# Half of a two-stage kernel's first loads issued by GpSimd, and a pair's tiles begun earlier and further apart

## The chip, the cores and the metric

The kernel runs on one core of a Trainium2 chip. The metric is the time of one execution in device microseconds. Engines: PE (TensorE, matrix products), DVE (VectorE), ACT (ScalarE), POOL (GpSimd) and SP (SyncE, which only issues transfers). Each takes its own instructions in program order and waits at an instruction whose semaphores are not yet there. SP, ACT and POOL each have a queue from which they issue DMA transfers.

## The reference

Eight batches of 576 positions, eight heads of 64. Attention runs inside chunks of 64 positions; then a low-rank mix over positions (U of 576x32, V of 32x576) and a ReLU block of width 2048 act on each position's 512 channels.

```python
def _attn_ref(q, k, v):
    B, H, S, D = q.shape            # 8, 8, 576, 64
    chunk = 64; nc = S // chunk
    q_c, k_c, v_c = (a.reshape(B, H, nc, chunk, D) for a in (q, k, v))
    scores = np.matmul(q_c, k_c.transpose(0, 1, 2, 4, 3)) / np.sqrt(D)
    scores = scores - np.max(scores, axis=-1, keepdims=True)
    attn = np.exp(scores)
    attn = attn / (np.sum(attn, axis=-1, keepdims=True) + 1e-09)
    return np.matmul(attn, v_c).reshape(B, H, S, D)

def _moe_ref(x, U, V, w_ch1, w_ch2):   # x: (8, 576, 512), heads side by side
    h = x.transpose(0, 2, 1) @ U @ V
    u = x + h.transpose(0, 2, 1)
    ch = np.maximum(u @ w_ch1, 0.0) @ w_ch2    # 512 -> 2048 -> 512
    return u + ch
```

U, V and the weights come as 64-bit floats and are rounded on the chip, by integer operations on their two words.

## The kernel before

**Tiling.** Batches go in four pairs of 1152 positions, nine tiles of 128 each. A tile's attention gives x; the low-rank mix turns x into u; three tiles form a group. For each group and each of 16 weight blocks of 128 hidden units, `hidden` (line 825) makes 12 products h (each operand is split into a high and a low part of fewer bits, three products of four), ACT and DVE make the ReLU's high and low part (lines 833 and 838), and `project_out` (line 851) adds 9 products into the three tiles' outputs. Such a *block* is 21 products of PE; there are 4 x 3 x 16 = 192. All weights stay in SBUF once they are rounded and split (lines 92 to 105, 372 and 375).

**The first part is planned.** The first pair's nine tiles, the rounding of U, V and the weights, and the first 32 blocks are written as a graph of operations (`Op`) with an engine, a cost and resources. `order` plays the graph through with these costs and gives one order of all instructions; each engine executes its share in that order. `LEAD` ranks the pieces: T tiles, U, V, W weight blocks, P the products with U, M the mixes, S the split of U. `transfer` adds a DMA issue. In this part each tile's q, k and v are loaded by SP (lines 416 and 420; v in four transfers of 64 KB: two chunks c and two halves e of the heads), after POOL's memset of v's column of ones (line 411). U comes in four transfers (lines 244 to 252), V in one (line 295). `GATES` says after which blocks the second pair's first two tiles begin in the same way; meanwhile ACT issues transfers that write the second pair's q and k to DRAM in another order (`permute`), which the later tiles read.

**The rest is an agenda.** From slot `FIRST` = 128 on, a block has four slots, and `at(s, ...)` puts work into slot s. `plan_tile` puts a later tile's steps around the slot s of its scores: its load at s - 9, the DVE transposes at s - 4, the v load at s + 1 (`Tile.load_v`, line 689), the exponentials' transpose and sums at s + 2, their way through DRAM (`put_ex`, line 737, at s + 3 and `get_ex`, line 744, at s + 6). The values (line 752) of a tile run in the slot of the next tile's scores; `chain` lists these slots, and `made[pr, t]` is the slot in which tile t's values run. `plan_proj` places the five products with U of a batch (lines 565 and 566), `plan_mix` the mixes: low rank, add, transpose, through DRAM (lines 795 and 801) and, ten slots after the start, the split (lines 814 and 815) on which the next pair's `hidden` waits. Slots before `FIRST` don't exist for the agenda; `plan_tile` moves a load or a transpose that would come earlier to `FIRST`.

Of the kernel before, what the change touches and what calls it, by code (L numbers as in the profile page):

```python
# [21 lines left out]
def kernel(  # L22
# [11 lines left out]
    nc = tc.nc  # L34
# [20 lines left out]
    XROOM = 3  # L55
    GATES = (14, 29)
    BLOCKS = [(hp, e, c) for hp in range(HP) for e in range(2) for c in range(2)]
# [74 lines left out]

    def transfer(run, kb, *after, eng="SP", us=0.5, take="", free="", gbs=232.0):
        q = "dq" if eng == "SP" else "pq"
        o = Op(eng, us, run, *after, take=take + " " + q, lat=1.2 if eng == "SP" else 2.9)
        return Op("DMA", kb * 1.024 / gbs, lambda: None, o, free=free + " " + q, lat=0.5)
# [100 lines left out]
    def u_ops():  # L237
        st = {}

        def load(z):  # L240
            if z == 0:
                words = st["words"] = wslot((10, 2 * R), U32, "uraw")
                nc.vector.memset(words[:, 4:6], 0)
                nc.sync.dma_start(words[:, 0:4], moe_U[0 : 4 * P].rearrange("(t p) r -> p t r", p=P))
                st["raw"] = words.rearrange("p t (r w) -> p t r w", w=2)
            words = st["words"]
            if z == 1:
                nc.sync.dma_start(words[0:C, 4], moe_U[4 * P : S])
            if z == 2:
                nc.sync.dma_start(words[C:P, 5], moe_U[0:C])  # L250
            if z == 3:
                nc.sync.dma_start(words[:, 6:10], moe_U[C:S].rearrange("(t p) r -> p t r", p=P))

        def spread():
            uf.append(wslot((10, 4, R), F32, "ufull"))
            nc.gpsimd.memset(uf[0][:, :, 3, :], 0.0)
            nc.scalar.copy(uf[0][:, :, 0:3, :], st["a"].unsqueeze(2).broadcast_to([P, 10, 3, R]))

        ld = None
        for z in range(4):  # L260
            ld = transfer(
                lambda z=z: load(z), (128, 16, 16, 128)[z], ld and ld.after[0], take="" if z else "w"
            )
        o, cv = rounding(Later(lambda: st["raw"]), lambda: wslot((10, R), U32, "uroom"), ld, "w", 10 * R)

        def keep():
            st["a"] = cv["a"].bitcast(F32)
            spread()

        return Op("ACT", 1.0, keep, o, take="w", free="w"), st  # L270
# [14 lines left out]
    def v_ops():  # L285
# [7 lines left out]
        def load():  # L293
            words = wslot((2 * n,), U32, "vraw")
            nc.sync.dma_start(words, moe_V.rearrange("r (b c) -> b r c", b=4))
            st["raw"] = words.rearrange("p (r w) -> p r w", w=2)
# [23 lines left out]

        ld = transfer(load, 147, take="w")
        o, _ = rounding(Later(lambda: st["raw"]), room, ld, "w", n)
# [77 lines left out]
    def load(pr, t, z):  # L400
# [12 lines left out]
        if z != "v":  # L413
            dst, src = (loaded[pr, t][0], q) if z == "q" else (loaded[pr, t][1], k)
            for r, m, b, s0 in segments(pr, t):
                nc.sync.dma_start(dst[r : r + m], src[b, :, s0 : s0 + m, :].rearrange("h s d -> s h d"))  # L416

    def load_v(pr, t, c, e):
        b, s0 = divmod(t * P + c * C, S)
        nc.sync.dma_start(  # L420
            loaded[pr, t][2][e * C : (e + 1) * C, c, :, 0:D],
# [3 lines left out]
    def attention_ops(pr, t, after=None):  # L425
# [88 lines left out]
        for c in range(2):  # L514
            for e in range(2):
                lv = transfer(
                    lambda c=c, e=e: load_v(pr, t, c, e),
                    64,
                    lv.after[0],
                    eng="SP",  # L520
                    us=0.5,
                )
# [141 lines left out]
    class Tile:  # L664
# [19 lines left out]
        def load_v(self):  # L684
            self.vn = slot(F32, "vn_" + self.n, (P, 2, HP, D))
            for c in range(2):
                b, s0 = divmod(self.t * P + c * C, S)
                for e in range(2):
                    nc.sync.dma_start(
                        self.vn[e * C : (e + 1) * C, c],  # L690
# [177 lines left out]
    def block_ops(pr, g, f, first, final, after, prev):  # L868
# [21 lines left out]
        for j in range(GT):  # L890
            d = Op("PE", 0.7, lambda j=j: out(j), c, d, take="bank" if first else "", free="h" if j == GT - 1 else "")
            if final:
                ends.append(
# [9 lines left out]

    LEAD = "T0 T1 T2 U T3 T4 W0 T5 P0 T6 V T7 T8 P1 M1 M0 W1 W2 W3 W4 W5 W6 W7 W8 W9 W10 M2 W11 W12 W13 W14 W15 S"
    STRETCHES = ((0, 0, 2), (1, 0, 4), (0, 2, 8), (1, 4, 12), (0, 8, 16), (1, 12, 16))
# [54 lines left out]
    manual.__enter__()  # L960
    for o in order():
        o.run()

# [13 lines left out]
    def at(s, *runs):  # L977
        agenda.setdefault(s, []).extend(runs)

    def plan_tile(pr, t, s, begin, end):  # L980

        a = Tile(pr, t)
        tile_of[pr, t] = a
        at(max(s - 9, begin), a.load)
        at(max(s - 4, begin), a.turn)
        at(s + 1, a.load_v)
# [13 lines left out]
    def plan_proj(pr, e, i, s):  # L1000
# [4 lines left out]
        at(s + 1, lo.run)  # L1005
        at(s + 4, product.run, *(z.run for z in rest))

    projs = {}
    tile_of = {}

    chain = [((1, t), FIRST + s) for t, s in zip(range(len(GATES), 7), (8, 18, 28, 38, 50))]
    for pr in range(1, NPAIR):
# [8 lines left out]
    for key, s in chain:  # L1021
        now = plan_tile(*key, s, FIRST, None) if key else None

# [15 lines left out]
    for pr in range(1, NPAIR):  # L1039
# [8 lines left out]
        for t in range(3):  # L1048
            plan_mix(pr, t, s + 7 + 2 * t)
        s = made[pr, 8] + 1  # L1050
        for i in range(5):
            plan_proj(pr, 1, i, s - 4 + i)
        for t in range(3, 6):
            plan_mix(pr, t, s + 7 + 2 * (t - 3))
        for t in range(6, 9):
            plan_mix(pr, t, base + NF * 4 + 6 + 8 * (t - 6))

    now = FIRST
    for pr in range(NPAIR):
# [46 lines left out]
```

## Time and profile before

| | |
|---|---|
| time, median of 3 runs | 958.88 us (956.23 to 963.89) |
| the profiled execution | 960.21 us, span 958.2 us |
| PE busy | 924.3 us, 96% |
| DVE, ACT, POOL busy | 452.5, 230.6, 1.7 us |
| DMA moved | 97.45 MB, mean 102 GB/s |
| PE's clock as granted | 0.989 of full speed over the run |

PE's busy time is modelled and includes what one product takes inside the array, so PE can be 100% busy; what counts is where it is not. In lists of waits a row gives the waiting engine and line, what it waited for, the total, the number of waits and the longest. "SPq" is SP's issue of a transfer, and "issue" stands where the trace shows no releaser.

### The profile page before, as it was taken

The numbers are of one execution on the slowest core, as the hardware profiler recorded it, in microseconds if no ns is written. First come the engines' busy times: TensorE is split into PE (matmuls) and PEld (weight loads), VectorE is DVE, ScalarE is ACT, GpSimd is POOL, SyncE is SP. The second block draws the span as 40 slices with busy tenths as digits, with TensorE's granted clock in tenths as the row PEclk, the third lists the DMA queues.
The fourth block names the chain that finished last, engine by engine and source line by source line (L and its number), as shares of the span: only waits on it lengthen the run. The fifth ranks groups of instructions, "written<-read, shape, count | busy, mean of one in ns | idle before, by whom it ended". The sixth has DMA issues, their size and how long they took to land.

```text
span 958.2 us, 16149 instructions
## 1 busy us (share of the span) xinstructions
PE 924.3 (96%) x6632; PEld 816.2 (85%) x6632; DVE 452.5 (47%) x890; ACT 230.6 (24%) x405; POOL 1.7 (0%) x18
## 2 busy tenths in 40 slices
PE   4789999999999999999999999999999999999998
PEld 3468988888888888888889888888889889899997
DVE  3669988144574455534632555543641533321211
ACT  3545655121221122112211121111221121111110
POOL 0000000000000000000000000000000000000000
PEclk8979999999999999999999999999999999999999
DMA  7792355456758634432764635442350312210000
GB/s 149 173 297 95 134 174 109 73 116 156 152 117 201 114 75 135 111 77 71 156 127 78 136 71 127 126 102 47 78 133 1 100 23 67 66 34 1 33 1 34
DMA packets 307005, 97.45 MB, mean 102 GB/s; under 512 B 239348, under 2 KB 296820, under 8 KB 306932
## 3 DMA queue, kind: packets, MB, share of 16 engines
q1 hardware_dynamic: 195572, 82.27, 33.3%
q10 hardware_dynamic: 111360, 14.16, 9.4%
q8 instruction: 52, 0.85, 0.4%
q14 instruction: 21, 0.17, 0.1%
HBM read 73.32 MB, written 37.22 MB: 115 GB/s over the span
## 4 chain that ended last, share of the span: by engine, by line
PE 88%; DMA 3%; DVE 3%; SPq 3%; ACT 1%; issue 1%; POOL 0%; DVEq 0%; ACTq 0%; POOLq 0%
PE h L825 41%; PE o L851 40%; PE as L752 2%; SPq L420 1%; PE as L699 1%; DMA qkv<-in_q_dram 1%; PE u L612 1%; PE ps_eT L433 1%; PE ut L624 1%; DMA vraw<-in_moe_V_dram 1%; PE y L566 1%; DMA wraw<-in_moe_w_ch_dram 1%; SPq L416 0%; PE av L482 0%; ACT hh L833 0%
## 5 line engine op out<-in xcount | busy, mean ns | idle before, releaser
L825 PE MATMUL h<-uth,w 128*128 128x384 f32 x1536 | 424.3, 339 | 1.3 <-ACT uth L814 1.3
L851 PE MATMUL o<-w,hh 128*128 128x512 f32 x1152 | 364.2, 397 | 0.0
L838 DVE SCALAR_TENSOR_TENSOR hl<-h,hh 128x384 fp32r<-128x384 f32 x192 | 106.9, 557 | 416.9 <-ACT hh L833 416.6
L825 PEld LDWEIGHTS h<-uth,w 128*128 128x128 f32 x1536 | 281.3, 188 | 9.6 <-ACT uth L814 1.8
L825 PE MATMUL h<-utl,w 128*128 128x384 f32 x768 | 260.0, 339 | 0.5 <-DVE utl L815 0.5
L851 PEld LDWEIGHTS o<-w,hh 128*128 128x128 f32 x1152 | 212.3, 188 | 35.9
L851 PE MATMUL o<-w,hl 128*128 128x512 f32 x576 | 227.4, 395 | 0.0
L833 ACT ACTIVATE hh<-h 128x384 fp32r<-128x384 f32 x192 | 94.3, 491 | 549.6 <-PE h L825 542.2
L825 PEld LDWEIGHTS h<-utl,w 128*128 128x128 f32 x768 | 144.3, 188 | 9.1 <-DVE utl L815 0.7
L851 PEld LDWEIGHTS o<-w,hl 128*128 128x128 f32 x576 | 108.4, 188 | 25.4
L863 DVE TENSOR_TENSOR x<-o,x 128x512 f32<-128x512 f32 x48 | 31.2, 680 | 3.4 <-PE o L851 3.4
L719 ACT ACTIVATE ex<-ex 128x512 f32<-128x512 f32 x25 | 15.8, 632 | 68.1 <-DVE ex L713 68.1
L712 DVE TENSOR_REDUCE mx<-as 128x4 f32<-128x256 f32 x50 | 20.9, 419 | 13.3 <-PE as L699 13.1
L618 DVE TENSOR_TENSOR x<-u,x 128x512 f32<-128x512 f32 x36 | 23.9, 678 | 4.7 <-PE u L612 4.7
L752 PEld LDWEIGHTS as<-vn,eT 64*64 64x64 f32 x800 | 15.5, 134 | 11.4 <-issue 10.5
L752 PE MATMUL as<-vn,eT 64*64 64x64 f32 x800 | 19.5, 225 | 2.9 <-issue 2.6
L815 DVE TENSOR_TENSOR utl<-uf,uth 128x512 fp32r<-128x512 f32 x27 | 18.5, 687 | 8.1 <-ACT uth L814 8.1
L713 DVE TENSOR_TENSOR ex<-as,mx 128x256 f32<-128x256 f32 x50 | 21.2, 425 | 1.7
L554 ACT CAST xh<-x 128x512 fp32r<-128x512 f32 x30 | 18.1, 615 | 14.4 <-DMA out_dram<-x 5.0
L375 DVE TENSOR_TENSOR w<-wroom,w 128x1024 fp32r<-128x1024 f32 (+1 forms) x19 | 20.0, 1051 | 1.3 <-ACT w L372 1.2
L372 ACT CAST w<-wroom 128x1024 fp32r<-128x1024 f32 (+1 forms) x19 | 17.2, 913 | 13.6 <-DVE wroom L105 13.5
L102 DVE SCALAR_TENSOR_TENSOR wraw<-wraw 128x1024 uint32<-128x1024 uint32 (+1 forms) x19 | 20.0, 1054 | 0.8 <-ACT wraw L95 0.8
(91 smaller groups left out, 509.7 us busy)
## 6 DMA issues: line engine op xcount, KB each, us to landing
wraw<-in_moe_w_ch_dram SPq DMA_DIRECT2D x32, 512.0 KB, 4.6
out_dram<-x SPq DMA_DIRECT2D x36, 256.0 KB, 2.2
vn<-in_v_dram SPq DMA_DIRECT2D x108, 64.0 KB, 2.4
qblocks<-in_q_dram ACTq DMA_DIRECT2D x24, 288.0 KB, 4.0
kblocks<-in_k_dram ACTq DMA_DIRECT2D x24, 288.0 KB, 3.9
xs<-xb SPq DMA_DIRECT2D x108, 64.0 KB, 1.8
uf<-xs SPq DMA_DIRECT2D x27, 256.0 KB, 2.8
exs<-exb SPq DMA_DIRECT2D x100, 64.0 KB, 1.8
```

Of the source, the lines that this page charges most:

```text
L102: lambda: nc.vector.scalar_tensor_tensor(lo, hi, 0x80000000, lo, op0=ALU.bitwise_and, op1=ALU.bitwise_or),
L375: nc.vector.tensor_sub(st["w"][:, 1, cols], v, st["w"][:, 0, cols])
L618: nc.vector.tensor_add(x, st["u"], x)
L712: nc.vector.reduce_max(mx[:, e], self.sc[e].rearrange("p (h k) -> p h k", k=C), axis=AX.X)
L713: nc.vector.tensor_sub(self.ex[:, e].rearrange("p b h k -> p h b k"), self.sc[e].rearrange("p (h b k) -> p h b k", b=2, k=TB), mx[:, e].un ...
L752: nc.tensor.matmul(ps[e][cs, (HP + hp) * C : (HP + hp + 1) * C], lhsT=self.eT[rows, hp, 2 * c : 2 * c + 2, :].rearrange("p a i -> p (a i)" ...
L815: nc.vector.tensor_sub(ul, self.uf, uh)
L825: nc.tensor.matmul(ps[:, :GN], lhsT=w[:, z, cc], rhs=u[:, cc, :], start=(n == 0), stop=(n == 3 * NCC - 1))
L833: nc.scalar.activation(hh, ps[:, :GN], AF.Relu)
L838: nc.vector.scalar_tensor_tensor(hl, ps[:, :GN], 0.0, hh, op0=ALU.max, op1=ALU.subtract)
L851: nc.tensor.matmul(acc[j], lhsT=h[:, js], rhs=w2[f][:, z], start=(first and i == 0), stop=(final and i == 2),)
L863: nc.vector.tensor_add(x, ps, x)
```

## The change

The loads of U and V, and in the first pair's tiles the two of four v transfers with c = 0, are issued on GpSimd's queue instead of SP's; so are all v transfers of the tiles on the agenda (`Tile.load_v`). The c = 0 transfers no longer stand behind k in the plan. `LEAD` takes V third and W0 later, and S before the last weights. The second gate comes five blocks earlier. The agenda now starts at slot 0 and is run between the planned blocks too, so the second pair's third tile has its scores at `FIRST` - 13, and the following tiles stand at `FIRST` + 2, 14, 27 and 42 instead of 18, 28, 38 and 50. The fifth product with U of each batch and all but a pair's last three mixes come one slot later after their tile. The planner's cost of an issue goes from 0.5 to 0.62 us.

```diff
-    GATES = (14, 29)
+    GATES = (14, 24)
...
-    def transfer(run, kb, *after, eng="SP", us=0.5, take="", free="", gbs=232.0):
+    def transfer(run, kb, *after, eng="SP", us=0.62, take="", free="", gbs=232.0):
...
-                nc.sync.dma_start(words[:, 0:4], moe_U[0 : 4 * P].rearrange("(t p) r -> p t r", p=P))
+                nc.gpsimd.dma_start(words[:, 0:4], moe_U[0 : 4 * P].rearrange("(t p) r -> p t r", p=P))
...
-            nc.sync.dma_start(words, moe_V.rearrange("r (b c) -> b r c", b=4))
+            nc.gpsimd.dma_start(words, moe_V.rearrange("r (b c) -> b r c", b=4))
...
-        nc.sync.dma_start(
+        (nc.gpsimd if early(pr, t) and c == 0 else nc.sync).dma_start(
             loaded[pr, t][2][e * C : (e + 1) * C, c, :, 0:D],
...
                     64,
-                    lv.after[0],
-                    eng="SP",
-                    us=0.5,
+                    (lk.after[0] if mine else lv.after[0]) if c else lq0,
+                    eng="SP" if c or not mine else "POOL",
...
-                    nc.sync.dma_start(
+                    nc.gpsimd.dma_start(
                         self.vn[e * C : (e + 1) * C, c],
...
-    LEAD = "T0 T1 T2 U T3 T4 W0 T5 P0 T6 V T7 T8 P1 M1 M0 W1 W2 W3 W4 W5 W6 W7 W8 W9 W10 M2 W11 W12 W13 W14 W15 S"
+    LEAD = "T0 T1 V T2 U T3 T4 T5 T6 W0 T7 P0 T8 M0 P1 M1 W1 W2 W3 W4 W5 S W6 W7 W8 W9 W10 M2 W11 W12 W13 W14 W15"
...
-        at(max(s - 9, begin), a.load)
-        at(max(s - 4, begin), a.turn)
+        at(s - 9, a.load)
+        at(s - 4, a.turn)
...
-        at(s + 4, product.run, *(z.run for z in rest))
+        at(s + (5 if i == 4 else 4), product.run, *(z.run for z in rest))
...
-    chain = [((1, t), FIRST + s) for t, s in zip(range(len(GATES), 7), (8, 18, 28, 38, 50))]
+    chain = [((1, t), FIRST + s) for t, s in zip(range(len(GATES), 7), (-13, 2, 14, 27, 42))]
...
-            plan_mix(pr, t, s + 7 + 2 * t)
+            plan_mix(pr, t, s + 8 + 2 * t)
...
-    now = FIRST
+    now = 0
+    for o in plan:
+        o.run()
+        if o.name == "out":
+            for z in range(2 if o.last else 1):
+                for run in agenda.pop(now, ()):
+                    run()
+                now += 1
+    assert now == FIRST
```

SP's queue from the program's first transfer, before (qkv is a first-pair tile's q, k and v; x4 stands for four transfers):

```order
L416 DMA qkv_0_84<-in_q_dram 128x8x64
L416 DMA qkv_0_84<-in_k_dram 128x8x64
L420 DMA qkv_0_84<-in_v_dram 64x4x64 x4
L416 DMA qkv_1_92<-in_q_dram 128x8x64
L416 DMA qkv_1_92<-in_k_dram 128x8x64
L420 DMA qkv_1_92<-in_v_dram 64x4x64 x4
L416 DMA qkv_2_131<-in_q_dram 128x8x64
L416 DMA qkv_2_131<-in_k_dram 128x8x64
L420 DMA qkv_2_131<-in_v_dram 64x4x64 x4
L244 DMA uraw<-in_moe_U_dram 128x4x64
```

now:

```order
L416 DMA qkv_0_84<-in_q_dram 128x8x64
L416 DMA qkv_0_84<-in_k_dram 128x8x64
L420 DMA qkv_0_84<-in_v_dram 64x4x64 x2
L416 DMA qkv_1_98<-in_q_dram 128x8x64
L416 DMA qkv_1_98<-in_k_dram 128x8x64
L420 DMA qkv_1_98<-in_v_dram 64x4x64 x2
L416 DMA qkv_2_120<-in_q_dram 128x8x64
```

and POOL's queue now, from the identity's first memset, which before held memsets and the AFFINE_SELECT alone here:

```order
masks.py:197 MEMSET ident 128x128
L411 MEMSET qkv_0_84 128x8
L295 DMA vraw<-in_moe_V_dram 128x1x288
L244 DMA uraw<-in_moe_U_dram 128x4x64
masks.py:199 ISA
masks.py:199 AFFINE_SELECT ident<-ident 128x128
L248 DMA uraw<-in_moe_U_dram 64x64
L420 DMA qkv_0_84<-in_v_dram 64x4x64 x2
L411 MEMSET qkv_1_98 128x8
L250 DMA uraw<-in_moe_U_dram 64x64
L252 DMA uraw<-in_moe_U_dram 128x4x64
L420 DMA qkv_1_98<-in_v_dram 64x4x64 x2
```

V, U and two v transfers of each tile have gone over; SP's rows of v have x2 instead of x4 and those of U are gone from it. The identity's AFFINE_SELECT stands behind two transfers, and tile 1's memset, on which SP's own v transfers of that tile wait, behind five.

ACT's queue at the start, before (uroom and vroom are the rounding of U and V, qkT a tile's transposed q and k, ex the exponentials, eT their transpose), from the first tile's eT on:

```order
L443 COPY eT_0_188<-ps_eT_0_163 128x512
L92 ACTIVATE uroom<-uraw 128x320
L95 ACTIVATE uraw<-uraw 128x320
L443 COPY qkT_2_241<-ps_qT_2_219 128x512
L443 COPY qkT_2_241<-ps_kT_2_233 128x512
L473 ACTIVATE ex_1_212<-ex_1_212 128x512
```

and now, from the first tile's qkT on:

```order
L443 COPY qkT_0_117<-ps_qT_0_103 128x512
L92 ACTIVATE vroom<-vraw 128x144
L443 COPY qkT_0_117<-ps_kT_0_112 128x512
L95 ACTIVATE vraw<-vraw 128x144
L443 COPY qkT_1_170<-ps_qT_1_152 128x512
L473 ACTIVATE ex_0_161<-ex_0_161 128x512
L314 CAST vst<-vall_166 128x288
L443 COPY qkT_1_170<-ps_kT_1_174 128x512
L443 COPY eT_0_198<-ps_eT_0_184 128x512
L314 CAST vst<-vall_195 128x288
L92 ACTIVATE uroom<-uraw 128x320
L95 ACTIVATE uraw<-uraw 128x320
```

V's rounding has moved from behind the seventh tile's q and k to the first tile; U's stands behind the first tile's eT in both.

SP's queue at the second pair's third and fourth tile (here _2 and _3; exs is `put_ex`, eT `get_ex`), before:

```order
L689 DMA vn_2_2315<-in_v_dram 64x4x64 x4
L674 DMA qn_3_2320<-qblocks_1532 128x4x128
L674 DMA kn_3_2321<-kblocks_1533 128x4x128
L737 DMA exs_2_2338<-exb_2_2328 32x4x128 x4
L744 DMA eT_2_2366<-exs_2_2338 128x4x32 x4
L689 DMA vn_3_2449<-in_v_dram 64x4x64 x4
L674 DMA qn_4_2454<-qblocks_1532 128x4x64
```

and now, with line numbers one lower:

```order
L736 DMA exs_2_2200<-exb_2_2190 32x4x128 x4
L743 DMA eT_2_2243<-exs_2_2200 128x4x32 x4
L673 DMA qn_3_2248<-qblocks_1531 128x4x128
L673 DMA kn_3_2249<-kblocks_1532 128x4x128
L865 DMA out_dram<-x_3_525 128x512
L865 DMA out_dram<-x_4_600 128x512
L865 DMA out_dram<-x_5_671 128x512
L736 DMA exs_3_2373<-exb_3_2359 32x4x128 x4
```

The v transfers have left the queue, and the third tile's rows now stand ahead of the outputs (line 865, 866 before) of the planned blocks.

More of the change, by code (lines that the diff above doesn't have):

```diff
@@ L247, in load @@
             if z == 1:
-                nc.sync.dma_start(words[0:C, 4], moe_U[4 * P : S])
+                nc.gpsimd.dma_start(words[0:C, 4], moe_U[4 * P : S])
             if z == 2:
-                nc.sync.dma_start(words[C:P, 5], moe_U[0:C])
+                nc.gpsimd.dma_start(words[C:P, 5], moe_U[0:C])
             if z == 3:
-                nc.sync.dma_start(words[:, 6:10], moe_U[C:S].rearrange("(t p) r -> p t r", p=P))
+                nc.gpsimd.dma_start(words[:, 6:10], moe_U[C:S].rearrange("(t p) r -> p t r", p=P))
         def spread():
@@ L261, in u_ops @@
             ld = transfer(
-                lambda z=z: load(z), (128, 16, 16, 128)[z], ld and ld.after[0], take="" if z else "w"
+                lambda z=z: load(z), (128, 16, 16, 128)[z], ld and ld.after[0], eng="POOL", take="" if z else "w"
             )
@@ L319, in low @@
             nc.vector.tensor_sub(dst, st[z][rows, 0 : 2 * n], dst)
-        ld = transfer(load, 147, take="w")
+        ld = transfer(load, 147, eng="POOL", take="w")
         o, _ = rounding(Later(lambda: st["raw"]), room, ld, "w", n)
@@ L413, in load @@
         if z != "v":
-            dst, src = (loaded[pr, t][0], q) if z == "q" else (loaded[pr, t][1], k)
+            dst, src = (loaded[pr, t][0], q) if z == "q" else (loaded[pr, t][1], k_in)
             for r, m, b, s0 in segments(pr, t):
@@ L891, in block_ops @@
             d = Op("PE", 0.7, lambda j=j: out(j), c, d, take="bank" if first else "", free="h" if j == GT - 1 else "")
+            d.name, d.last = "out", j == GT - 1
             if final:
@@ L960 @@
     manual.__enter__()
-    for o in order():
-        o.run()
+    plan = order()
     pend = None
@@ L978, in at, with plan_tile @@
         agenda.setdefault(s, []).extend(runs)
-    def plan_tile(pr, t, s, begin, end):
+    def plan_tile(pr, t, s):
         a = Tile(pr, t)
-        tile_of[pr, t] = a
-        at(max(s - 9, begin), a.load)
-        at(max(s - 4, begin), a.turn)
+        at(s - 9, a.load)
+        at(s - 4, a.turn)
         at(s + 1, a.load_v)
@@ L1005, in plan_proj @@
         at(s + 1, lo.run)
-        at(s + 4, product.run, *(z.run for z in rest))
+        at(s + (5 if i == 4 else 4), product.run, *(z.run for z in rest))
     projs = {}
-    tile_of = {}
-    chain = [((1, t), FIRST + s) for t, s in zip(range(len(GATES), 7), (8, 18, 28, 38, 50))]
+    chain = [((1, t), FIRST + s) for t, s in zip(range(len(GATES), 7), (-13, 2, 14, 27, 42))]
     for pr in range(1, NPAIR):
@@ L1021 @@
     for key, s in chain:
-        now = plan_tile(*key, s, FIRST, None) if key else None
+        now = plan_tile(*key, s) if key else None
         def both(prev=prev, now=now):
@@ L1053 @@
         for t in range(3, 6):
-            plan_mix(pr, t, s + 7 + 2 * (t - 3))
+            plan_mix(pr, t, s + 8 + 2 * (t - 3))
         for t in range(6, 9):
             plan_mix(pr, t, base + NF * 4 + 6 + 8 * (t - 6))
-    now = FIRST
+    now = 0
[7 more added lines that the diff above has]
+    assert now == FIRST
     for pr in range(NPAIR):
```

## The prediction

> **What bounds the kernel now.** I read the page's busy times first, then busy time by stretches, then what TensorE (PE) waited for.
>
> ```profile
> span 958.2 us, 16149 instructions
> PE 924.3 (96%) x6632; PEld 816.2 (85%) x6632; DVE 452.5 (47%) x890; ACT 230.6 (24%) x405; POOL 1.7 (0%) x18
> PE   4789999999999999999999999999999999999998
> ```
>
> ```profile
> 0.00:80.00 80.00, 57.17 (x775) 42.52 (x776) 47.26 (x118) 38.12 (x65) 1.63 (x17) 0.87 0.76 200
> 80.80:210.00 129.20, 129.20 (x742) 116.30 (x742) 89.06 (x129) 62.09 (x90) 0.11 (x1) 1.00 0.50 121
> 217.00:298.00 81.00, 76.35 (x631) 66.89 (x629) 44.46 (x96) 16.11 (x30) 0.00 (x0) 1.00 0.73 153
> ```
>
> Each row: the stretch, its length, then busy time of PE, PE's weight loads, DVE, ACT and POOL, the granted clock, the DMA share and GB/s. PE is the bound. From 80.8 to 210 it never idles, so nothing off PE can be worth anything there. It idles 80.00 - 57.17 = 22.8 us in the first 80 us, and 81.00 - 76.35 = 4.7 us while the second pair's attention is prepared. PE's own waits over the whole span, in total, times, longest:
>
> ```profile
> PE ps_qT L433 <- DMA qkv<-in_q_dram: 7.7, 4, 4.2
> PE sc L451 <- ACT qkT L443: 6.8, 2, 6.1
> PE ps_eT L433 <- ACT ex L473: 5.8, 3, 3.1
> PE y L566 <- DVE xl L558: 2.7, 5, 0.7
> PE as L752 <- issue: 2.6, 3, 1.2
> PE ut L624 <- DVE x L618: 1.8, 1, 1.8
> PE h L825 <- ACT uth L814: 1.3, 1, 1.3
> PE y L571 <- DVE x L500: 0.8, 1, 0.8
> PE h L825 <- DVE utl L815: 0.5, 1, 0.5
> ```
>
> They add to 30.0 us. The five on lines 433, 451, 624 and 571 add to 22.9: that is the start's whole idle time. The other four, 7.1 us, lie in the later stages. Who holds ACT, on which PE waits at the start, is seen in ACT's waits of the first 82 us:
>
> ```profile
> ACT uroom L92 <- DMA uraw<-in_moe_U_dram: 6.4, 1, 6.4
> ACT wroom L92 <- DMA wraw<-in_moe_w_ch_dram: 5.1, 2, 4.0
> ACT vroom L92 <- DMA vraw<-in_moe_V_dram: 3.5, 1, 3.5
> ```
>
> ACT works in order: while it waits for U or V to land, the copies and exponentials that PE needs stand behind. These loads are late because SP issues everything:
>
> ```profile
> 0.73 0.44 SPq L416 DMA_DIRECT2D qkv<-in_q_dram  x1
> 49.05 4.09 SPq L420 DMA_DIRECT2D qkv<-in_v_dram  x4
> 53.25 0.54 SPq L347 DMA_DIRECT2D wraw<-in_moe_w_ch_dram  x1
> L420 SPq DMA_DIRECT2D qkv<-in_v_dram x36: 596/616/3241, 1.9 to 51.5; - x36
> DMA to landing us min/median/max: 2.3/3.3/6.1
> ```
>
> The last two are the v loads of the first pair: issue in ns (least, median, most), and time to landing. The row at 53.25 is the second weight block. Counted in the program, 63 transfers stand ahead of it: 56 for the nine tiles (six each, two more for the tile that crosses the batches), U's four, V's one, two for the first weight block. (53.25 - 0.73) / 63 = 0.83 us each.
>
> **The start, part by part.** SP loses 18 v transfers (two of four in nine tiles), U's four and V's one: 40 remain, at 0.83 us 33.2 us instead of 52.5. What they cost on GpSimd's queue the trace cannot show: it has no such transfer. The bounds are the least and the most of the very same v transfer on SP, 0.60 and 3.24 us; I take twice its median, 1.2 us, because another engine makes the issue, and keep both ends. To land I give them SP's 3.3 us. Work begins at about 1 us and the identity's AFFINE_SELECT takes 0.3.
>
> New waits come with it. SP's first v transfer of each tile waits for a POOL memset of the ones column, and that memset now stands behind POOL transfers. Tile 1's stands behind five (V, two of U, two of v): 1 + 0.3 + 5 x 1.2 = 7.3 us. SP arrives after six issues, at 0.73 + 6 x 0.62 = 4.5, and waits 2.8 us, with tile 2's q and k queued behind. Tile 2's stands behind nine: 12.1 us, against 7.3 + 4 x 0.62 = 9.8, a wait of 2.3. At tile 3 it is eleven, 14.5 against 12.1 + 2.5 = 14.6, so no more. SP then reaches the second weight block at 0.73 + 33.2 + 5.1 = 39 us, 14 us earlier. The identity, on which the first transpose depends, stands behind two transfers: 1 + 2.4 + 0.3 = 3.7 us, inside the first wait for q (4.2); nothing, while at 3.24 us it would be 7.8 and cost 3.6.
>
> What PE gets of it, wait by wait:
> - The 6.1 us at line 451 came through ACT from U. U's last part is now the seventh POOL transfer: 1 + 0.3 + 7 x 1.2 + 3.3 = 13.0 us, and ACT takes up U behind the first tile's eT copy, as before:
>
> ```profile
> 12.65 0.58 ACT L443 COPY eT<-ps_eT 128x512 f32<-128x512 f32 x1 [0.73 <-PE ps_eT L433]
> ```
>
>  That ends at 13.2. I count 5.5.
> - The waits for q but the first: 7.7 - 4.2 = 3.5, gone, since each q is issued earlier.
> - Of 5.8 at line 433 behind the exponentials, 5.8 - 3.1 = 2.7 is nearly all behind V's landing; V now lands within 6 us of the start: 2.4.
> - The 3.1 us came behind ACT's 4.0 for the second weight block. ACT still takes that block up between two tiles' work, but it is issued 14 us earlier while the work ahead of it ends some 10 earlier: half, 1.5.
>
> Together 12.9. The 1.8 (a DVE queue) and the 0.8 stay. I take back 2.4, one wait of V's size, for a stall in the new order that I don't see: **10.5 us**. The cover then is the DVE: the second weight block was ready just before PE used it.
>
> ```profile
> 78.97 1.21 DVE L375 TENSOR_TENSOR w<-wroom,w 128x1024 fp32r<-128x1024 f32 x1
> 80.85 0.44 PE L825 MATMUL h<-uth,w 128*128 128x384 f32 x1
> 80.00:140.00 60.00, 60.00 (x307) 54.44 (x306) 58.32 (x70) 40.51 (x48) 0.00 (x0) 1.00 0.38 120
> ```
>
> 80.18 against 80.85, and DVE is busy 58.32 of the next 60 us: the start's gain holds only if DVE's weight work moves forward too. It has 80 - 47.26 = 32.7 us idle before that, so I let it.
>
> **The second pair, part by part.** SP's queue around the first such tile, the chain there, and the steady pace of blocks at the end:
>
> ```profile
> 232.56 3.51 SPq L744 DMA_DIRECT2D eT<-exs  x4
> 236.12 2.63 SPq L689 DMA_DIRECT2D vn<-in_v_dram  x4
> DMA to landing us min/median/max: 2.1/2.2/4.1
> ...
> 236.66 1.20 issue
> 292.25 3.53 DMA uf<-xs
> ...
> 939.88 2.12 PE h L825 x12
> 944.09 2.11 PE h L825 x12
> ```
>
> (The landing row is that of eT, line 744.) eT's last piece is issued at about 235.6 and lands 2.2 later, at 237.8; PE's stall at line 752 ends at 236.66 + 1.20 = 237.86. So these three stalls (2.6 us) are eT coming late. A block takes 944.09 - 939.88 = 4.21 us, a slot a quarter of it, 1.05. The tiles stood 10, 10, 10, 12 and 20 slots apart; now 15, 12, 13, 15 and 28. Two slots more are 2.1 us, above the longest stall of 1.2. The four v transfers (2.63 us) leave SP too, so the next tile's put and get no longer queue behind them. 2.6 goes. On POOL four v transfers at 1.2 are 4.8 us, and even at 3.24 they are 13, about the 12 slots (12.6 us) that they have.
>
> PE's 1.3 and 0.5 at line 825 are the next pair's first block waiting for its split input, behind the uf transfer of the row at 292.25. The tile that ends the first batch is used at slot FIRST + 27 instead of FIRST + 38, and the mixes start one slot later after it: 10 slots, 10.5 us earlier. Both go: 1.8. The 2.7 at line 566 is the fifth product of a batch waiting for its low part, at most 0.7 each; it now runs one slot later, 1.05 us: it goes.
>
> That is 7.1. I take back 0.6, half the longest of these stalls, because the tiles begun earlier share PE's planned blocks with the last weights: **6.5 us**. PE's work itself is the same: the program has the same matmuls.
>
> **Two rules of the Trainium skill.** DVE's clamp on the weights, line 101, beside a two-input operation of the same shape, line 102:
>
> ```profile
> L101 DVE TENSOR_SCALAR wroom<-wroom x19: 417/686/696, 35.0 to 159.9; 128x1024 f32<-128x1024 f32 x13, 128x512 f32<-128x512 f32 x6
> L102 DVE SCALAR_TENSOR_TENSOR wraw<-wraw x19: 682/1218/1240, 36.0 to 160.8; 128x1024 uint32<-128x1024 uint32 x13, 128x512 uint32<-128x512 uint32 x6
> 0.00:53.25 53.25, 35.32 (x557) 25.84 (x558) 27.15 (x76) 25.37 (x46) 1.63 (x17) 0.87 0.73 161
> ```
>
> 0.69 against 1.22 us: the clamp runs in a faster mode. The Trainium skill ("SBUF — State Buffer", SBUF: two separate sides) says that such a DVE operation holds a port that GpSimd needs to write descriptors, so transfers issued there stall till it ends. By that rule each clamp costs GpSimd at most its 0.69 us; one weight clamp falls into the first 53 us, so the sum would be 0.7 smaller at worst; no GpSimd transfer is in this trace to show it. The other rule is the second rival below.
>
> **The rivals.** (1) *GpSimd's issue becomes the bound, slower than before.* Tile 8's v is POOL's 23rd transfer. At x us each it is issued by 1 + 23x, against 49.05 + 4.09 = 53.14 now. The start's gain is cut from x = (53.14 - 10.5 - 1) / 23 = 1.8 on, is gone at 2.3, the whole change at 2.27 + 6.5 / 23 = 2.55, and it is 1% slower (9.6 us, about what a measurement of this kernel can tell from no change) at 2.97. At 3.24 the last v comes at 75.5, 22.4 late: 958.88 + 22.4 - 6.5 = 974.8. For it: one v transfer on SP did take 3.24. Against: its median is 0.62, and 23 in a row would all have to be slow. (2) *The DMA engines are the bound.* To 53.25 us they moved 161 GB/s, 8.57 MB, at a share of 0.73. If that cannot rise, the start gains nothing: 958.88 - 6.5 = 952.4; at full share, 161 / 0.73 = 220 GB/s, the bytes need 39 us, as early as SP now gets there. Between: 948. The Trainium skill ("DMA: Bandwidth & Descriptors", Issuing engines are not separate DMA queues) says that this is what spreading issue over engines meets: the same 16 engines, only issue time saved. The row, with 0.27 of the share free, speaks for room. (3) *DVE's weight work does not move forward*, and PE meets the second weight block where it did: again 952.4.
>
> **How the numbers follow.** The profiled execution took 960.21 us, 2.0 more than its span and 1.3 more than the median of 958.88. 960.21 - 10.5 - 6.5 = 943.2 for a like execution, 958.88 - 17.0 = **941.9** for the median. Chances: this forecast 0.70; DMA engines 0.08, half of it beyond 1% faster (below 949.3); DVE 0.06, within 1%; GpSimd between 1.8 and 2.97 us 0.08, half faster, half within 1%; GpSimd slower still 0.06; better than forecast by the full 18.7 us of the start (22.9 less the first 4.2) and 7.1, 933, 0.02. Faster 0.80, same 0.14, slower 0.06. The forecast's own range is 936 to 948. From 934 to 955 the range holds it with the DMA and DVE cases and GpSimd up to about 2.6 us; beyond it lie the slow GpSimd cases.
>
> **What would show it.** Right: PE's 6.1 at the scores and the waits on line 433 but the first are gone, the second weight block is issued near 39 us, steady PE begins near 70 instead of 80.8, no stall at the values of the second pair's tiles or at that pair's first block. Wrong: transfers on POOL's queue of 2 us or more, SP waiting for POOL's memsets throughout the nine tiles; a DMA share that stays near 0.73; or PE waiting for the DVE's weights between 70 and 130 us.

## The result, and the profile after

The changed kernel took 949.97 us (median of 4 runs, 949.36 to 951.59), the kernel before beside it 960.31 (4 runs, 956.23 to 963.89): a ratio of 0.9896, 95% interval 0.9852 to 0.9940. The profiled execution took 949.82 us with a span of 948.0, against 958.2. So 10.2 us went from the span where 17.0 were forecast. In the experiments below, with 13 runs of the kernel before in each group, the changed kernel run again was 8.5 us faster (0.9911); the kernel before was profiled in one of its longer runs, so differences of spans against it come out 1 to 3 us larger than those of times. The page of the changed kernel, its span and busy times:

```profile
span 948.0 us, 16316 instructions
PE 920.9 (97%) x6632; PEld 814.4 (86%) x6632; DVE 452.0 (48%) x890; ACT 229.5 (24%) x405; POOL 77.8 (8%) x141
```

Busy time by stretches shows where the 10.2 us came from. First the kernel before, then the changed one: from the start to block 1 of the weights (the point where PE begins to run without a pause), from there to block 32, and on to block 48, the next pair's first. By block 48 both have done the same work of PE.

```profile
0.00:80.80 80.80, 57.97 (x779) 43.04 (x779) 48.06 (x120) 38.58 (x66) 1.63 (x17) 0.87 0.75 198
80.80:217.20 136.40, 136.40 (x805) 122.39 (x804) 92.46 (x138) 63.45 (x92) 0.11 (x1) 1.00 0.48 114
217.20:297.40 80.20, 75.75 (x630) 66.58 (x628) 43.66 (x95) 16.11 (x30) 0.00 (x0) 1.00 0.73 153
```

```profile
0.00:69.50 69.50, 53.91 (x780) 39.80 (x780) 47.28 (x120) 39.12 (x67) 16.64 (x40) 0.95 0.98 231
69.50:207.50 138.00, 137.76 (x836) 122.89 (x837) 96.67 (x148) 62.57 (x92) 4.99 (x9) 1.00 0.52 124
207.50:289.30 81.80, 76.29 (x597) 67.95 (x596) 40.31 (x85) 15.29 (x29) 9.76 (x16) 0.96 0.68 142
```

The start is 80.80 - 69.50 = 11.3 us shorter. From block 1 to block 48 the time grew by (138.00 + 81.80) - (136.40 + 80.20) = 3.2 us. The rest of the run, 958.2 - 297.4 = 660.8 before and 948.0 - 289.3 = 658.7 now, gives 2.1. Together 11.3 - 3.2 + 2.1 = 10.2: the start did what was forecast, and the second pair's part, forecast at 6.5 us, gave nothing but a small loss.

Two columns of the rows say more. In the start PE's idle time fell from 22.83 to 15.59 us, by 7.2; the other 4.1 us are PE's busy time for the same work (779 and 780 instructions), 57.97 to 53.91, with a granted clock of 0.95 instead of 0.87. And the DMA share of the start rose from 0.75 to 0.98. PE's waits in the first 80 us now (waiting engine and line, releaser, total, times, longest):

```profile
PE ps_qT L433 <- DMA qkv<-in_q_dram: 7.4, 3, 4.2
PE sc L451 <- ACT qkT L443: 3.1, 2, 2.4
PE ps_kT L433 <- DMA qkv<-in_k_dram: 2.0, 2, 1.1
PE ps_eT L433 <- ACT ex L473: 1.6, 2, 1.4
```

and PE's waits between 205 and 300 us:

```profile
PE as L751 <- DMA eT<-exs: 3.9, 2, 3.0
PE as L698 <- DVE kT L681: 1.6, 1, 1.6
```

Before, the eT stalls of this stage were 2.6 us in three, and the scores (line 698) had none. The 1.3 and 0.5 us of the next pair's first block are gone. So a new and larger stall stands where the old ones were. The chain of waits at it, in order of time:

```profile
205.41 0.54 SPq L673
...
205.99 5.21 DMA kn<-kblocks
211.22 0.71 DVE kT L681
...
219.64 0.43 SPq L736
...
220.11 0.66 SPq L673
...
220.88 0.56 SPq L673
...
222.16 0.63 SPq L673
...
222.97 0.65 SPq L743
...
224.76 4.20 DMA eT<-exs
```

Line 736 is the put of a tile's exponentials, 743 their get, 673 the loads of a later tile's q and k. The tile is late from its own k on, issued behind a get at 205.41: PE stands 1.6 us for its scores. Then four q and k transfers stand on SP between the put and the get: the get begins 2.9 us after the put has been issued (220.07 to 222.97), and in the two kernels below in which nothing stands between them 1.0 after it. Its last piece takes 4.20 us to land (median of this transfer 2.6). These are 1.9 and 1.6 us, and PE stands for 3.0 and 0.9.

### The profile page after: what moved, and what is told of

The parts are those of the page before. It is cut to its first block, busy times and chain, and to the rows that moved or that the text cites. A ratio compares the mean times of both kernels' runs of the same rounds, so it can differ in the third digit from the quotient of the medians.

```text
span 948.0 us, 16316 instructions
## 1 busy us (share of the span) xinstructions
PE 920.9 (97%) x6632; PEld 814.4 (86%) x6632; DVE 452.0 (48%) x890; ACT 229.5 (24%) x405; POOL 77.8 (8%) x141
## 4 chain that ended last, share of the span: by engine, by line
PE 88%; DVE 4%; DMA 3%; SPq 2%; issue 1%; POOL 1%; ACT 0%; ACTq 0%; DVEq 0%; POOLq 0%
PE h L824 41%; PE o L850 40%; PE as L751 2%; PE as L698 1%; DMA qkv<-in_k_dram 1%; DMA qkv<-in_v_dram 1%; DMA eT<-exs 1%; PE u L611 1%; PE y L565 1%; SPq L736 1%; PE y L564 1%; DVE x L617 1%; DMA kn<-kblocks 1%; SPq L743 1%; PE av L482 0%
## 5 line engine op out<-in xcount | busy, mean ns | idle before, releaser
L688 POOL DMA_DIRECT2D vn<-in_v_dram x100 | 61.1, 618 | 549.6 <-PE y L565 141.7
L681 DVE STREAM_TRANSPOSE qT<-qn 128x512 f32<-128x512 f32 x25 | 17.5, 701 | 11.7 <-DMA qn<-qblocks 10.2
```

Source lines behind the costliest of these rows:

```text
L688: nc.gpsimd.dma_start(self.vn[e * C : (e + 1) * C, c], v[b + 2 * self.pr, HP * e : HP * (e + 1), s0 : s0 + C, :].rearrange("h s d -> s h d"),)
```

## Experiments

Each was timed in three rounds beside the kernel before, four kernels to a chip (before's median 957.06, 957.54 and 958.98 us in the three groups). The starts of blocks are read from the first product h of each block; "32 to 48" is the time between those two blocks.

| kernel | median us | ratio, interval | block 32 at | 32 to 48 | span |
|---|---|---|---|---|---|
| before (profile) | 958.88 | 1 | 217.2 | 80.2 | 958.2 |
| changed (profile) | 949.97 | 0.9896, 0.9852-0.9940 | 207.5 | 81.9 | 948.0 |
| changed again | 948.59 | 0.9911, 0.9877-0.9945 | 207.6 | 81.9 | 947.8 |
| start alone | 952.46 | 0.9947, 0.9930-0.9964 | 206.1 | 80.4 | 949.6 |
| pair alone | 957.79 | 1.0003, 0.9988-1.0018 | 216.3 | 81.3 | 956.4 |
| loads first | 942.77 | 0.9847, 0.9832-0.9862 | 207.1 | 74.4 | 940.8 |
| loads first, again | 943.66 | 0.9839, 0.9811-0.9866 | 207.8 | 75.6 | 943.5 |
| loads last | 952.37 | 0.9934, 0.9909-0.9959 | 207.2 | 85.5 | 950.9 |
| v on SP | 947.72 | 0.9897, 0.9882-0.9912 | 208.4 | 79.9 | 946.7 |
| loads first, v on SP | 944.94 | 0.9877, 0.9841-0.9914 | 209.7 | 77.2 | 945.6 |
| U and V only | 955.35 | 0.9972, 0.9954-0.9991 | 213.6 | 81.0 | 953.6 |
| long pieces | 943.95 | 0.9860, 0.9826-0.9893 | 202.1 | 80.8 | 941.6 |
| all v on GpSimd | 955.91 | 0.9971, 0.9956-0.9986 | 220.1 | 74.1 | 954.3 |
| V later | 950.37 | 0.9915, 0.9892-0.9938 | 216.1 | 74.0 | 948.8 |

**The two halves of the change.** *Start alone*: the start as in the changed kernel, the later tiles as before.

```diff
-    chain = [((1, t), FIRST + s) for t, s in zip(range(len(GATES), 7), (-13, 2, 14, 27, 42))]
+    chain = [((1, t), FIRST + s) for t, s in zip(range(len(GATES), 7), (8, 18, 28, 38, 50))]
...
-                    nc.gpsimd.dma_start(
+                    nc.sync.dma_start(
```

(the second is in `Tile.load_v`; gates and the slots of mixes and fifth products also as before)

> The start's loads on GpSimd with the new ranking, and the second pair's tiles, gates, agenda and v loads as in the kernel before. Theory (the start earns all of it; the second pair's part trades old stalls for new ones of the same size): steady PE begins near 69.5 us, the old stalls of 5.7 us between 217 and 350 us are back, and the time is 947 to 950 us, the changed kernel's own. Rival (the second pair's part earns its 6.5 us and the start the remaining 4): 955 to 957 us.

*Pair alone*: the start as before, the later tiles as in the changed kernel.

> The second pair's part alone (second gate at block 24, agenda among the planned blocks, wider spacing, v of the later tiles on GpSimd); U, V and all first-pair v loads on SP and the old ranking. Theory (the start earns all): steady PE begins near 80.8 us, stalls of some 7 us at the third and fourth tile of the second pair, time 957 to 961 us. Rival (this part earns 6.5): 952 to 954 us.

By timing the start alone gains 5.1 us (0.9947) and the pair's part alone nothing (1.0003). Pair alone falls into its theory's range; start alone, at 952.46, lies in neither, so the theory that the start earns all of it missed by 2.5 us. Against the changed kernel's 8.5 to 10.0 us the two halves alone are some 4 us short. Start alone has the old stalls back in the second pair's stage:

```profile
PE as L751 <- issue: 1.7, 2, 0.9
PE h L824 <- ACT uth L813: 1.7, 1, 1.7
PE as L751 <- DMA eT<-exs: 0.7, 1, 0.7
```

By the traces it is 2.8 us ahead of the changed kernel at block 48 (286.5 against 289.3), and then needs 663.1 us to the end where the changed kernel needs 658.7 and pair alone 658.7: PE waits for that block's split input as before, and its clock is at 0.88 in the 14 us from 286. So the start gives the greater part of the gain. The second half takes the old stalls away, and with the new start the time behind block 48 is 4.4 us shorter for it; ahead of that block it puts other stalls in their place.

**What makes eT late.** *Loads first*: the changed kernel, with the q and k loads of the second pair's fourth to seventh tile one slot after the previous tile's scores, ahead of its put.

```diff
-        at(s - 9, a.load)
+        at(s - ahead, a.load)
...
+        ahead = s - last - 1 if key and key[0] == 1 and 3 <= key[1] <= 6 else 9
```

> The changed kernel with the q and k loads of the second pair's fourth to seventh tile put one slot after the scores of the tile before, so ahead of that tile's way through DRAM on SP's queue. Theory (the loads, placed nine slots before their tile, now stand in SP's queue beside and ahead of the exponentials' return, and cost the stalls of 1.6, 3.0 and 0.9 us): these three go, 4 to 7 us faster than the changed kernel, 943 to 946 us. Rival (v transfers on GpSimd's queue, landing at the same time, slow the return): the stalls stay, 949 to 951 us.

942.77 us, 5 to 6 us less than the changed kernel by the ratios (0.9847 against 0.9896 and 0.9911), with nothing else altered, and the fastest of all. Of the three stalls only 0.7 us at eT is left. SP's queue then, where four q and k loads stand ahead of the put (214.57) and the get (218.26):

```profile
209.35 0.52 SPq L673 DMA_DIRECT2D qn<-qblocks  x1
...
211.31 0.63 SPq L673 DMA_DIRECT2D kn<-kblocks  x1
214.57 2.73 SPq L736 DMA_DIRECT2D exs<-exb  x4
218.26 2.04 SPq L743 DMA_DIRECT2D eT<-exs  x4
```

and the stage from block 32 to 48, to be held against the changed kernel's row of 207.50:

```profile
207.10:281.50 74.40, 73.73 (x598) 65.73 (x597) 39.62 (x85) 15.29 (x29) 9.80 (x16) 1.00 0.73 148
```

81.80 - 74.40 = 7.4 us: idle time falls from 5.51 to 0.67, and PE's busy time for the same work from 76.29 to 73.73, at a clock of 1.00 instead of 0.96. So the stalls cost half as much again in PE's busy time. The changed kernel's slices from the stall for eT on (PE stands from 224.77 to 227.76, and 0.9 us more up to 229.10):

```profile
224.00:227.70 3.70, 0.77 (x4) 0.30 (x2) 1.79 (x3) 0.00 (x0) 1.71 (x3) 0.98 1.22 202
228.00:234.50 6.50, 5.60 (x74) 5.03 (x74) 2.27 (x6) 0.63 (x1) 0.00 (x0) 0.51 0.05 8
235.00:240.00 5.00, 5.00 (x27) 4.56 (x26) 2.18 (x6) 0.53 (x2) 0.00 (x0) 1.00 0.71 125
```

The granted clock is halved just behind the stall, for some 6.5 us, though PE works through most of them, and is full again from 235 on.

Loads first moves the loads ahead of the put and also makes them earlier. *Loads last* tells these apart from the other side: the same four tiles' loads seven slots after the previous scores, behind the get.

```diff
-        at(s - 9, a.load)
+        at(s - ahead, a.load)
...
+        ahead = s - last - 7 if key and key[0] == 1 and 3 <= key[1] <= 6 else 9
```

> The changed kernel with the same four tiles' q and k loads two slots AFTER the scores' put and get of the previous tile's exponentials have been passed on SP (seven slots after its scores, in place of nine before its own). Theory: only the order on SP matters, and each side loses when it is behind; here eT is ahead and its stalls (3.0 and 0.9) go, while q and k come late, so the stall at the scores (PE on DVE's kT, 1.6 us once) grows to 1 to 4 us at several tiles: 947 to 952 us. Rival: only the delay of eT cost anything, and q and k have room; then no stalls above 0.7 us and 942 to 944 us, as with the loads first.

PE's waits between 205 and 300 us:

```profile
PE as L698 <- DVE kT L681: 6.5, 3, 3.1
PE as L751 <- DMA eT<-exs: 0.5, 1, 0.5
```

eT's stall is all but gone and the scores' stall has taken its place, 6.5 us in three, and 952.37 us in all. The rival falls: q and k had no room behind the get. Here, whichever of the two stands behind on SP is late; only ahead of the put did both have room. *Loads first, again* was run beside it:

> The kernel with the second pair's q and k loads ahead of the previous tile's put, once more, as the common measure for the runs beside it: 942 to 944 us, block 1 at 69 to 71 us, stalls of at most 0.7 us between 205 and 290 us.

943.66 us, with eT stalls of 1.9 us in this profile where the first had 0.7; two executions of one kernel differ by that much here.

**Was GpSimd's queue any help to the later tiles?** *v on SP*: the changed kernel with `Tile.load_v` on `nc.sync` again.

> The changed kernel with the v loads of the later tiles back on SP. Theory (SP's order, not the v transfers, sets the stalls): SP's queue is 2.6 us longer per tile, the stalls at the fourth and fifth tile stay or grow by up to 2.6 us each, 950 to 955 us. Rival (v transfers on GpSimd's queue slow the exponentials' return): stalls shrink by 2 us or more, 945 to 948 us.

947.72 us, ratio 0.9897, no worse than the changed kernel. The theory missed (950 to 955), and the rival's numbers came: stalls were 0.6 at the scores and 2.7 at eT, 2.2 us less than the changed kernel's 1.6 and 3.9. With the loads where the change puts them, GpSimd's queue brought v nothing; that it slows the exponentials' return is not shown by this. With both edits:

> Both earlier edits together: the q and k loads of the second pair's fourth to seventh tile ahead of the previous tile's put, and the later tiles' v back on SP. Theory: only the place of the loads on SP mattered, and the queue of v is then nearly indifferent, 941 to 944 us, as with the loads moved alone (942.8). Rival 1: v on GpSimd costs something by itself (putting it back gave 2.3 us when the loads stood late); then another 1 to 2.5 us go, 940 to 942. Rival 2: v on SP stands ahead of the put of its own tile (four issues, 2.5 us) and makes eT late again; then stalls of 1 us and more for eT come back and it is 945 us or more.

944.94 us, between the theory and its second rival. PE stands 2.0 us for eT; loads first had 0.7 and 1.9. The ratio's interval, 0.9841 to 0.9914, overlaps those of both runs with v on GpSimd. So the queue that v is on is worth at most about 2 us here, and these runs don't settle its sign.

**What bounds the start.** *U and V only*: all of the first pair's v transfers back on SP.

```diff
-        (nc.gpsimd if early(pr, t) and c == 0 else nc.sync).dma_start(
+        nc.sync.dma_start(
...
-                    (lk.after[0] if mine else lv.after[0]) if c else lq0,
-                    eng="SP" if c or not mine else "POOL",
+                    lv.after[0],
+                    eng="SP",
```

> The changed kernel with all v transfers of the first pair's tiles back on SP; U and V alone are issued by GpSimd. Theory: of the start's gain (block 1 from 80.8 to 69.5 us) the part that came through U and V on ACT stays (forecast at 5.5 and 2.4 us), and the part that came from SP's shorter queue (q waits 3.5, half of the weights' wait 1.5) goes: block 1 at 73 to 76 us, about 953 to 956 us. Rival: the DMA engines are full in this stage whoever issues, so which queue the v transfers are on is indifferent: block 1 at 69 to 71 us and 949 to 951 us.

955.35 us. The planner puts block 1 ahead of the last pause in this kernel (69.0 us, and block 2 at 79.6), so block 32 is the measure: 213.6, against 207.6 in the changed kernel beside it and 216.3 in pair alone. Of 8.7 us, U and V, with the new ranking that comes with them, bring 2.7 and the v halves 6.0. The theory holds in its total, but not in its split: it gave the greater part to U and V. With v on SP the waits for q grow to 9.4 us:

```profile
PE ps_qT L433 <- DMA qkv<-in_q_dram: 9.4, 4, 4.2
```

*Long pieces*: the changed kernel, with the first pair's q and k read as rows of 2 KB that lie together, in place of eight pieces of 256 bytes a row. These are other positions' numbers, so this kernel leaves out the right result of the first pair.

```diff
+                if early(pr, t):
+                    rows = src[b].rearrange("h s d -> (h s d)").rearrange("(r c) -> r c", c=DM)
+                    nc.sync.dma_start(dst[r : r + m].rearrange("p h d -> p (h d)"), rows[s0 : s0 + m])
+                    continue
```

> The changed kernel, but the first pair's nine tiles read q and k as rows of 2 KB that lie together in DRAM, in place of eight pieces of 256 bytes per row: the same transfers, bytes and order, other positions' data (so the first pair's attention is that of other numbers). Theory: in the changed kernel's first 45 us the 16 DMA engines are full (share 1.01 at 186 GB/s) because of the short pieces; with long ones the share falls below 0.9, SP's issues take 0.6 us again, the second weight block is issued before 41 us (45.07 now) and block 1 starts 2 to 6 us before 69.5. Rival: the engines were full only by the way and the start is bound by the order of work on PE, ACT and DVE; then the share falls too, but block 1 starts at 68.5 to 70 us and the time stays within 1.5 us of the changed kernel's.

943.95 us against 948.59 beside it, block 1 at 64.1 instead of 69.4. Up to the issue of the second weight block, first in the changed kernel run beside it (44.72 us), then in this one (36.38 us):

```profile
0.00:44.72 44.72, 33.03 (x527) 24.70 (x528) 23.16 (x73) 24.17 (x45) 16.62 (x40) 0.92 1.05 187
```

```profile
0.00:36.38 36.38, 26.07 (x480) 19.58 (x480) 20.18 (x64) 20.77 (x40) 16.65 (x40) 1.00 1.00 230
```

The same transfers pass in 8.3 us less, at 230 instead of 187 GB/s. The theory holds in its time; that the share would fall below 0.9 was wrong, since the engines stay full and only carry more. So the 256-byte pieces on full DMA engines set the pace of the loads in the changed kernel's start. The Trainium skill ("DMA: Bandwidth & Descriptors", Why small descriptors are slow (HBM only)) says that of the cycles that a piece of 256 bytes takes a DMA engine 27% are overhead; the traces agree in kind, with 230 / 187 = 1.23 where only q and k were lengthened. How the 5.3 us at block 1 came to PE shows in the rows up to there, first the changed kernel's, then this one's:

```profile
0.00:69.40 69.40, 54.73 (x780) 39.98 (x780) 47.29 (x120) 39.18 (x67) 16.62 (x40) 0.95 1.00 231
0.00:64.10 64.10, 50.88 (x779) 37.17 (x779) 47.23 (x120) 38.82 (x67) 16.65 (x40) 1.00 0.91 250
```

Idle time fell by 14.67 - 13.22 = 1.4 us, and PE's busy time for the same work by 3.9, at a clock of 1.00 instead of 0.95.

Durations of SP's k issues (least, median, most, in ns), in the kernel before, in the changed kernel and with long pieces:

```profile
L416 SPq DMA_DIRECT2D qkv<-in_k_dram x10: 566/581/633, 1.2 to 48.4; - x10
```

```profile
L416 SPq DMA_DIRECT2D qkv<-in_k_dram x10: 571/1332/1972, 1.2 to 42.1; - x10
```

```profile
L418 SPq DMA_DIRECT2D qkv<-in_k_dram x10: 327/430/538, 1.2 to 33.2; - x10
```

The issue of k takes 0.58 us at the share of 0.75 of before, 1.33 with the same pieces on full engines, and 0.43 with long pieces on full engines. That of q stays at 0.60 with both; why only some issues stretch is not shown.

*All v on GpSimd*: loads first, with all four v transfers of each early tile on GpSimd.

```diff
-        (nc.gpsimd if early(pr, t) and c == 0 else nc.sync).dma_start(
+        (nc.gpsimd if early(pr, t) else nc.sync).dma_start(
...
-                    (lk.after[0] if mine else lv.after[0]) if c else lq0,
-                    eng="SP" if c or not mine else "POOL",
+                    lv.after[0] if c else lq0,
+                    eng="POOL" if mine else "SP",
```

> Loads first as before, and in the first pair all four v transfers of a tile on GpSimd in place of two, so SP has 18 issues less ahead of the weights. Theory: the DMA engines are full in the first 45 us, so fewer issues on SP bring nothing: share 1.0 and the second weight block issued no more than 2 us before 45, block 1 at 68 to 71 us, 941.5 to 944.5 us. Rival: issue on SP still bounds the start (18 transfers at 0.62 us); then the second weight block is issued 5 us or more earlier and block 1 starts at 62 to 66 us, 936 to 940 us.

955.91 us, 12 more than loads first beside it: both were wrong. The second weight block is issued at 36.18 us as the rival said, and it brings nothing, as the theory said, but block 2 comes at 81.1 instead of 72.1. GpSimd's timeline shows why:

```profile
36.25 0.36 POOL L256 MEMSET ufull<- 128x320 f32 x1 [11.35 <-PE sc L451]
36.72 4.87 POOL L420 DMA_DIRECT2D qkv<-in_v_dram  x8
...
```

A memset of `ufull` waits 11.35 us for PE's scores, which by the program hold its buffer, and 15 v transfers stand behind it, the last issued by 48.6 us. In the changed kernel that memset waited for nothing (at 16.39 us), and six stood behind it. The planner also made another order of everything after it, so the whole 12 us are not put down to this wait; that 15 transfers had to wait behind it is shown.

*V later*: loads first, with V behind U and the fourth tile in `LEAD`.

```diff
-    LEAD = "T0 T1 V T2 U T3 T4 T5 T6 W0 T7 P0 T8 M0 P1 M1 W1 W2 W3 W4 W5 S W6 W7 W8 W9 W10 M2 W11 W12 W13 W14 W15"
+    LEAD = "T0 T1 T2 U T3 V T4 T5 T6 W0 T7 P0 T8 M0 P1 M1 W1 W2 W3 W4 W5 S W6 W7 W8 W9 W10 M2 W11 W12 W13 W14 W15"
```

> Loads first as before, and V's load and rounding behind U's and the fourth tile in the plan (third in the changed kernel). In the changed kernel ACT waits 2.1 us for V between the first tile's q and k copies, and PE 2.4 us for the scores behind it. Theory: this wait is on the path and nothing takes its place; block 1 1.5 to 2.5 us earlier than in the run beside it, 940 to 942 us. Rival: with full DMA engines the next q or k is late anyway, so PE waits there instead: block 1 within 1 us of the run beside it and the same time.

950.37 us, 6.7 more than beside it. The wait at the first scores did fall, from 2.3 to 0.7 us, and block 2 came at 72.1 us in both, so nothing was gained there, as the rival said. The loss, which neither foresaw, lies behind it, in a stage that the edit does not name; block 2 to block 32, first this kernel, then loads first beside it:

```profile
72.10:216.10 144.00, 137.51 (x826) 120.18 (x825) 94.13 (x146) 61.68 (x90) 5.00 (x9) 1.00 0.52 123
```

```profile
72.10:207.80 135.70, 135.46 (x824) 120.63 (x823) 94.94 (x147) 61.97 (x91) 4.99 (x9) 1.00 0.54 130
```

PE idles 6.5 us there, against 0.2, behind DVE and ACT. With one rank in `LEAD` changed, the planner gave another order of everything after it.

## Why the prediction was right or wrong

The forecast of 941.9 us was 8 us too low. Faster was right: by 1.04%, and 0.89% in the repeat, so both intervals lie below 1, and whether the gain reaches 1% stays open. The time lies outside the forecast's own range of 936 to 948, and inside the wider one of 934 to 955 that took in the cases of the DMA engines and the DVE. The start's term came out right in sum, but not in its parts; the second pair's did not come.

*The start's 10.5 us* measured 11.3 by the spans, out of parts that differ:

- *GpSimd's issue at 1.2 us*: 0.62, the value of the same transfer on SP. The bound from below, 0.60, was the right end, and the first rival, which needed 1.8 us, falls:

```profile
L420 POOL DMA_DIRECT2D qkv<-in_v_dram x18: 617/617/645, 3.9 to 22.1; - x18
```

- *SP's waits for POOL's memsets, 2.8 and 2.3*: 0.5 at tile 1, and none at tiles 2 and 3; with an issue of 0.62 in place of 1.2 the prediction's own sums give next to nothing. The list of SP's waits has 4.2 us in three, the longest 2.9, but two of these are not such waits: tile 2's memset was done before SP came to that tile's v, and tile 3's as well (10.91 against 17.67). The 2.9 us lies within the v issue itself, and a v issue took up to 3.24 before as well.

```profile
SPq L420 <- POOL qkv L411: 4.2, 3, 2.9
...
8.95 0.13 POOL L411 MEMSET qkv<- 128x8 f32 x1
...
12.05 3.57 SPq L420 DMA_DIRECT2D qkv<-in_v_dram  x2
```

- *U's 5.5*: the wait through U is gone, and V's took its place on ACT, which now waits for V ahead of the first tile's k copy; PE stands 2.4 us at the first scores. The 2.4 taken back "for a stall in the new order that I don't see" has this one's size, by luck: it was not foreseen.
- *The waits for q but the first, 3.5, gone*: wrong. They are 7.4 - 4.2 = 3.2, and k brings 2.0 more. Most q are issued earlier, but they land later: 5.6 us after their issue in the median, against 4.1 before.
- *V's 2.4 and the weights' 1.5* were right together: line 433 behind the exponentials fell from 5.8 to 1.6.
- *The 1.8 and the 0.8 stay*: the first is gone, of the second 0.4 is left; 2.2 better.
- *The second weight block near 39 us*: 45.07. Less 0.5 of waits, 40 transfers took (45.07 - 0.73 - 0.5) / 40 = 1.10 us each, not 0.83. The step took SP's mean issue for a fixed price of SP, and it grew with the load on the engines.
- What no step counted: PE's clock. 4.1 of the 11.3 us are the same work at 0.95 instead of 0.87. The idle time itself fell by 7.2, not by 10.5.

*The second rival*, the DMA engines as the bound, was right as a mechanism and sized too mildly: "at full share, 161 / 0.73 = 220 GB/s". To 45 us the changed kernel is at full share and moves 186 GB/s:

```profile
0.00:45.07 45.07, 32.43 (x527) 24.63 (x528) 23.40 (x73) 24.40 (x45) 16.64 (x40) 0.92 1.01 186
```

Share and rate were not in proportion here. The transfers ahead of the second weight block are the same 63 in both kernels, but a megabyte took the engines longer when two queues ran at once. SP's queue in the 53.25 us of before, then SP's and GpSimd's in these 45.07 (packets, MB, share):

```profile
q1 hardware_dynamic: 30262, 8.50, 72.7%
```

```profile
q1 hardware_dynamic: 23291, 6.70, 80.8%
q0 software_dynamic: 880, 1.63, 19.7%
```

0.727 x 53.25 / 8.50 = 4.6 us of the 16 engines for a megabyte before, and 5.4 now on either queue, although GpSimd's moves larger packets. This rival did not take the start's gain away, but it set its end, as long pieces shows. Its time, 948 to 952.4, holds the measured one by luck: it kept the second pair's 6.5 us, which did not come. The sentence of the Trainium skill cited there (the same 16 engines, only issue time saved) agrees with these rows. The Trainium skill's other rule cited there, that DVE's clamp stalls GpSimd's transfers, does not show where the two met. V's clamp fell into the issue of a v transfer that had begun 0.1 us earlier, in the changed kernel's timeline:

```profile
8.35 0.62 POOL L420 DMA_DIRECT2D qkv<-in_v_dram  x1 [1.22 <-DMA vraw<-in_moe_V_dram]
...
8.45 0.23 DVE L101 TENSOR_SCALAR vroom<-vroom 128x144 f32<-128x144 f32 x1 [4.62 <-ACT vroom L92]
```

The transfer took 0.62 us, the median of all. The first weight clamp comes at 43.8 us, when GpSimd issues no such transfer, so a longer overlap, or a transfer begun under a clamp, was not seen.

*The third rival*, DVE's weight work, did not come: PE has no wait on DVE's weights between 70 and 130 us.

*The second pair's 6.5 us* became a loss of 3.2 to block 48 and a gain of 2.1 behind it. The first block's 1.8 is gone, as said. The fifth products' 2.7 fell to 1.3, half of what was said. What failed is the step "Two slots more are 2.1 us, above the longest stall of 1.2. The four v transfers (2.63 us) leave SP too, so the next tile's put and get no longer queue behind them." It moved the tile and priced the v transfers, but not the next tile's q and k, which are planned at s - 9. With tiles 15, 12 and 13 slots apart that is 6, 3 and 4 slots after the previous scores, where its put (3) and get (6) stand. At 10 slots it had been one after the scores, ahead of the put; 2.6 us of stalls became 3.9 for eT and 1.6 for kT, and a slower clock on top. Loads first, which puts them back there, has 212.4 us from block 1 (69.1) to block 48 (281.5), against 216.6 before and 219.8 in the changed kernel; with 1.5 us behind block 48 (660.8 - 659.3) that is a gain of 5.7 in place of 6.5. Its second profile gives 3.7 (69.8 to 283.5, and 660.0 behind). So most of the term was there to be had, and one line kept it back.

## What to carry to other kernels

When a step is moved, list every transfer that is planned relative to it and see which others it passes on its queue: two slots more for a tile carried the next tile's loads from ahead of a put to behind it, and cost more than they gave. Ahead of a put and get that stand on the path, independent loads belong first, as long as they have a buffer. Spreading issue over two engines ended at the DMA engines here: before taking an issue's mean, or a rate scaled to full share, as a price, allow for both getting worse as the engines fill.

## What was unexpected in the hardware

- A v transfer (64 KB in 256-byte pieces) is issued by GpSimd in 0.617 us, the same as SP's 0.616, and landed in 3.0 us in the later stages against SP's 2.4 before.
- With full DMA engines SP's issue of k stretched from 0.58 to 1.33 us in the median (0.77 in start alone), while that of q did not. A single v issue took up to 3.75 us, and up to 3.24 before.
- A megabyte of the start's loads, most of it in 256-byte pieces, took the 16 engines 4.6 us at a share of 0.73 and 5.4 at full share.
- Behind a PE stall of 3.0 us, with 0.9 more just after it, the granted clock was halved for some 6.5 us; 360 instructions of that stage took 40.29 us of PE instead of 37.63. In the start PE's busy time fell by 4.1 us at the higher clock, more than half of what the idle time gave.

```profile
207.50:253.30 45.80, 40.29 (x360) 35.64 (x359) 23.35 (x53) 8.39 (x16) 4.88 (x8) 0.93 0.60 123
```

```profile
207.10:245.40 38.30, 37.63 (x360) 33.38 (x359) 22.27 (x51) 8.51 (x16) 4.91 (x8) 1.00 0.65 134
```
